# A shift convolution on the two row halves of TensorE's array, with one constant loaded later and some copies assigned by hand

## The chip, the cores and the metric

One core of one Trainium2 chip runs the whole program. The metric is device time in microseconds of one execution; the median of three runs is given, and one further execution was taken with the profiler. Engines are named as in the profile: PE is TensorE (PEld its weight loads), DVE is VectorE, ACT is ScalarE, POOL is GpSimd, SP is SyncE, which here only issues DMAs.

## The reference

The program computes four residual layers over a sequence of S = 2048 rows and D = 448 channels, and all gradients. Only the first kind of layer matters here:

```python
def _A_ref(q, k, v, shift_k, ssm_k, ssm_D):
    k_shift = jnp.zeros_like(k)
    for t in range(ks):                                   # ks = 4
        k_shift = k_shift + k_pad[:, t:t + S, :] * shift_k[:, ks - 1 - t][None, None, :]
    kv = k_shift * v
    y = irfft(rfft(kv) * rfft(ssm_k))[:S]                 # long causal convolution, by channel
    y = y + kv * ssm_D
    return q * y
x = x + A(layernorm(x)); x = x + B(layernorm(x)); x = x + A(layernorm(x)); x = x + B(layernorm(x))
```

`kv` and `y` don't depend on x, so they are computed once, in a prefix, and used by both A layers.

## The kernel before

**Stages.** `_ssm_prefix` computes `y` (tile Ysb) and stores what the backward pass needs: KS_d (the shifted k), and SPEC_d (the two spectra, of K and of KV). `Main.run` does the four layers and their backward pass in four chunks of 512 rows, with an order for PE written out by hand. `_ssm_suffix` does the backward pass of the convolution, with weight gradients (`Jobs`) woven in.

**The prefix**, in program order:

1. SP loads, one behind the other: the filter K in four parts (ksb), the constant M1sb in two halves, k (kn), v (vn), the first rows of x (x0c0), Gsb, Gpre, and Minvsb (1 MB, `_load_minv`, L389), which is first used by `ys` (L594), the last step of the prefix.
2. `k_turn` (L399) transposes K on PE, 16 transposes for 128 channels, and copies the result from PSUM in two halves. Which engine copies is chosen by `bal.pick`, which keeps a running sum of work given to ACT and DVE. `k_stage1` (L409) is the first FFT stage, four matmuls and one cast for each pair of rows.
3. The diagonals (L426): for each of 4 channel blocks of 112 and each of 4 taps, DVE scales the identity by the tap's column, so that a matmul with the result multiplies each channel by its tap. The taps are loaded by ACT's queue (skb) and cast to FP32 on POOL (skc).
4. SP turns two pieces of the K spectrum by DMA (L439) and, behind them, w2 (L449, L450), whose tile takes the place of kn.
5. k is transposed on PE (ps_kT, L445), 4 blocks of 112 channels for each of 16 row groups, and copied to kT by ACT (blocks 0 and 1) and DVE (blocks 2 and 3).
6. `conv(h, jq)` (L453): for half h of the channels (224) and four row groups, 4 x 2 x 4 = 32 matmuls of a 112x128 piece of kT with a 112x112 diagonal, four taps accumulated. ACT casts the result to SBUF (ks), POOL stores it to KS_d, DVE multiplies it with v (kvt). `stage1_kv` (L472) is the first FFT stage of kvt, two steps behind conv. Between them stand the turns of K's spectrum (h = 0) or `spec_k` (h = 1): the second FFT stage of K, its store to SPEC_d and four copies on POOL's queue that swap halves (KAB<-KAB).
7. The products, in the order of the string PRODUCTS, which fixes PE, ACT, DVE and POOL: second stages (P, F), turns of KV (Z), spectra products (M), inverse stages (V), casts, and on POOL the stores of both spectra. Two of the stores are followed by the loads of w1 (L556) and w2 (L562).
8. `ys` (L588) makes Ysb. `Main.run` weaves it with the first transposes and matmuls; the first chunk's X (L716) is written into the buffer that ZkvB had (tag WX), Ysb into that of ZkvA (tag W2).

**Rules that set the order.** PE, ACT and DVE copies of one PSUM tile run one after the other. `issue_after(i)` keeps what follows behind instruction i in the order of issue. A tile with the tag of an earlier one waits until all users of that one, DMAs included, are through. Each engine issues its DMAs in order; POOL's wait for earlier ones of its own to land before they reuse a semaphore. PSUM tag "A" has four buffers of two banks (4 KB in each partition).

`GBLK`, which exists before, is the list of channel blocks (0, 128), (128, 256), (256, 384), (320, 448): the last two overlap, and rows 64 to 127 of the last are channels 384 to 447.

Of the kernel before, what the change touches and what calls it, by code (L numbers as in the profile page):

```python
# [10 lines left out]
FP32 = mybir.dt.float32  # L11
BF16 = mybir.dt.bfloat16
# [5 lines left out]
P = 128  # L18
# [124 lines left out]
def kernel(  # L143
# [197 lines left out]
def _ssm_prefix(k):  # L341
# [4 lines left out]
    with ExitStack() as es:  # L346
# [19 lines left out]
        diag = w2o[:DC, 2 * S:].rearrange("p (c j d) -> p c j d", c=ND, j=4)  # L366
        kn = k.wk.tile([P, J, D], BF16, name="k_n", tag="WY")
        vn = k.wk.tile([P, J, D], BF16, name="v_n", tag="WB")
        skc = spec.tile([DC, ND, 4], FP32, name="skc")
        skb = spec.tile([DC, ND, 4], BF16, name="skb")  # L370
# [69 lines left out]
        for jq in range(4):  # L440
            pt = psum.tile([DC, ND, 4, P], BF16, name="ps_kT", **a_)
# [9 lines left out]
        DH = D // 2  # L451

        def conv(h, jq):  # L453
            ds = slice(h * DH, (h + 1) * DH)
            pc = psum.tile([P, 4, 256], FP32, name="ps_cv", tag="A", bufs=4)
            for u in range(4):
                j = 4 * jq + u
                for e in range(2):
                    for t in range(4):
                        js = (j - t) % J  # L460
                        src = kT[:, js // 4, 2 * h + e, js % 4, 1:129] if j >= t else kT[:, js // 4, 2 * h + e, js % 4, 0:128]
                        nc.tensor.matmul(pc[:, u, e * DC:(e + 1) * DC], lhsT=src, rhs=diag[:, 2 * h + e, t, :], start=(t == 0), stop=(t == 3))
            kk = work.tile([P, 2, 4, DH], BF16, name="ks_kv", tag="pab", bufs=4)
            ks, kvt = kk[:, 0], kk[:, 1]
# [3 lines left out]
            nc.vector.tensor_tensor(out=kvt, in0=ks, in1=vn[:, 4 * jq:4 * jq + 4, ds], op=ALU.mult)  # L468
            bal.add("dve", 0.62)
            return kvt  # L470

        def stage1_kv(h, jq, kvt):  # L472
            for u in range(0, 4, 2):
                n2 = 4 * jq + u
                ps = psum.tile([P, 2, 2, 256], FP32, name="ps_s1", **k.pt["s1"])
                for w in range(2):
                    for c in range(2):
                        nc.tensor.matmul(ps[:, w, c, :DH], lhsT=k.M1sb[:, n2 + w, c, :], rhs=kvt[:, u + w, :], start=True, stop=True)
                _copy(nc, bal.pick(4 * DH), A1kv[:, 112 * h:112 * (h + 1), :, n2:n2 + 2, :].rearrange("p b c w s -> p w c b s"),
                      ps[:, :, :, :DH].rearrange("p w c (b s) -> p w c b s", s=2))  # L480

# [713 lines left out]
def _ssm_suffix(k):  # L1195
# [8 lines left out]
    with ExitStack() as es:  # L1204
# [73 lines left out]
        for cp in range(NCI // 2):  # L1278
# [18 lines left out]
            if cp == 5:  # L1297
                ksf = sp.tile([P, 2, J, D // 2], BF16, name="ksf")
                with tc.issue_after(k.last_x.ins):
                    nc.scalar.dma_start(out=ksf[:], in_=k.KS_d[:].rearrange("h p j d -> p h j d"))  # L1300
# [24 lines left out]
        for i in range(8):  # L1325
# [8 lines left out]
            nc.vector.tensor_tensor(out=gks[:, sl, :], in0=gkv, in1=gks[:, sl, :], op=ALU.mult)  # L1334
            nc.vector.tensor_tensor(out=gkv.rearrange("p j (h d) -> p j h d", h=2), in0=gkv.rearrange("p j (h d) -> p j h d", h=2), in1=ksf[:, :, sl, :].rearrange("p h j d -> p j h d"), op=ALU.mult)
            nc.gpsimd.dma_start(out=out3_pm[:, sl, :], in_=gkv)
# [98 lines left out]
```

## Time and profile before

| | us |
|---|---|
| median of three runs (694.54 to 697.23) | 696.32 |
| profiled execution | 694.42 |
| its span, first to last instruction | 692.5 |
| PE busy | 672.4 (97%) |
| DVE / ACT / POOL busy | 481.5 / 429.2 / 104.6 |
| one conv on PE (32 matmuls) | 1.74 |
| first ps_y on PE | 86.0 |
| first matmul of the first layer's ps_h | 97.6 |

A line of the order of time gives start and duration in us, engine, line of the kernel, operation, tile written and tiles read, shape, count, and in brackets the engine's idle time before it and what ended that. A line of the table by stretch gives the stretch and its length, busy time and number of instructions of PE, PEld, DVE, ACT and POOL, TensorE's granted clock, the share of the 16 DMA engines in use and what they moved in GB/s; the share counts packets by their durations, so overlapping packets can take it above 1. The prefix in stretches of four microseconds begins so, and its first loads keep the DMA engines full:

```profile
0.00:4.00 4.00, 2.81 (x7) 1.01 (x8) 0.27 (x1) 1.49 (x2) 1.74 (x9) 1.00 0.40 127
4.00:8.00 4.00, 4.00 (x36) 3.03 (x35) 2.67 (x15) 0.00 (x0) 0.20 (x1) 1.00 1.03 360
...
16.00:20.00 4.00, 3.72 (x46) 3.29 (x45) 3.73 (x4) 4.00 (x6) 0.00 (x0) 1.00 1.00 411
...
24.00:28.00 4.00, 3.48 (x124) 3.13 (x122) 1.94 (x4) 3.63 (x3) 0.59 (x1) 1.00 1.47 167
28.00:32.00 4.00, 2.62 (x62) 2.46 (x62) 2.23 (x4) 2.92 (x4) 0.55 (x1) 0.84 0.99 252
```

### The profile page before, as it was taken

To read this page: it belongs to the slowest core of one execution; us is meant where nothing else is said; L and a number is where in the kernel's file an instruction comes from. 1 tells how busy PE (TensorE), PEld (TensorE's weight loads), DVE (VectorE), ACT (ScalarE), POOL (GpSimd) and SP (SyncE) were. 2 spreads that over 40 slices of the span, in tenths; PEclk is the share of its full clock that TensorE was granted. 3 is DMA by queue.
4 is the path that set the end of the run, shared out by engine and by line. 5 is a ranking of instruction groups with operands and counts; after the bars stand their busy time and mean duration, and the time that the engine had idled before them with its cause. 6 is when DMAs were issued, how large, how long until landed. Compare 5 with 4: busy or idle time off the path is not lost.

```text
span 692.5 us, 14496 instructions
## 1 busy us (share of the span) xinstructions
PE 672.4 (97%) x5879; PEld 363.3 (52%) x5879; DVE 481.5 (70%) x1131; ACT 429.2 (62%) x522; POOL 104.6 (15%) x177
## 2 busy tenths in 40 slices
PE   8899999899999999999999999999999999999997
PEld 6886845454434444444444444544554555555666
DVE  6579943667889858899478874843946555538992
ACT  5888976968847858669577685223543554554431
POOL 1057310110011100111000100010111211102311
PEclk9999999999999999999999999999999999999999
DMA  8999978269789877498666789949599988956981
GB/s 314 282 277 307 345 205 205 77 169 271 175 251 240 216 185 182 132 250 226 193 156 189 204 198 369 273 160 214 185 249 316 355 274 316 351 186 221 315 315 42
DMA packets 203956, 162.60 MB, mean 235 GB/s; under 512 B 153505, under 2 KB 184244, under 8 KB 203122
## 3 DMA queue, kind: packets, MB, share of 16 engines
q1 hardware_dynamic: 190806, 113.35, 60.2%
q0 software_dynamic: 11088, 39.84, 16.6%
q10 hardware_dynamic: 1996, 8.49, 3.6%
q8 instruction: 46, 0.75, 0.4%
q14 instruction: 20, 0.16, 0.1%
HBM read 66.05 MB, written 54.60 MB: 174 GB/s over the span
## 4 chain that ended last, share of the span: by engine, by line
PE 64%; DVE 18%; issue 6%; DMA 5%; ACT 4%; POOL 3%; POOLq 0%; ACTq 0%
PE ps_d L1077 24%; PE ps_n L867 8%; PE ps_h L669 6%; PE ps_g L669 6%; PE ps_o L829 5%; DVE ln_st L308 2%; DVE lb_v L1025 2%; PE ps_v L272 2%; POOL rstd L313 2%; DMA spec_KV<-ZkvB 1%; DVE n L316 1%; DVE lb_v L1028 1%; DVE lb_v L1029 1%; DVE X L833 1%; PE ps_h L673 1%
## 5 line engine op out<-in xcount | busy, mean ns | idle before, releaser
L1077 PEld LDWEIGHTS <-dstat 128*128 128x128 bf16 x928 | 87.0, 98 | 76.2 <-issue 4.0
L867 PE MATMUL ps_n<-w1T,ghT 128*128 128x448 bf16 x448 | 96.6, 353 | 2.0 <-DVE ghT L852 1.7
L829 PE MATMUL ps_o<-w2sb,aT 128*128 128x448 bf16 x448 | 89.2, 353 | 0.6 <-DVE X L833 0.6
L669 PE MATMUL ps_h<-nT,w1sb 128*128 128x512 bf16 (+1 forms) x420 | 84.4, 337 | 1.6 <-ACT Dall L116 1.0
L116 ACT CAST ghT<-ps_g 128x1024 bf16<-128x1024 f32 (+1 forms) x54 | 48.4, 899 | 58.3 <-PE ps_g L673 46.6
L669 PE MATMUL ps_g<-nT,w2T 128*128 128x512 bf16 x336 | 79.5, 379 | 1.0 <-DVE Dall L117 0.5
L867 PEld LDWEIGHTS <-ghT 128*128 128x128 bf16 x448 | 41.5, 98 | 50.6 <-DVE ghT L852 6.7
L829 PEld LDWEIGHTS <-aT 128*128 128x128 bf16 x448 | 43.2, 98 | 41.1 <-issue 2.7
L669 PEld LDWEIGHTS <-w1sb 128*128 128x128 bf16 x420 | 39.2, 98 | 36.7 <-issue 7.2
L812 ACT ACTIVATE aT<-ps_h 128x1024 bf16<-128x1024 f32 (+1 forms) x48 | 44.2, 921 | 19.4 <-PE ps_h L669 12.2
L116 ACT CAST Dall<-ps_h 128x1024 bf16<-128x1024 f32 (+2 forms) x60 | 54.3, 904 | 0.0
L1025 DVE SCALAR_TENSOR_TENSOR lb_v<-lb_u,n 128x448 bf16<-128x448 bf16 x60 | 37.2, 620 | 24.5 <-ACT lb_u L871 24.1
L313 POOL TENSOR_TENSOR rstd<-ln_ve,mhalf 128x2 f32<-128x2 f32 (+1 forms) x24 | 19.9, 831 | 225.3 <-DVE ln_ve L312 225.3
L669 PEld LDWEIGHTS <-w2T 128*128 128x128 bf16 x336 | 31.3, 98 | 42.0 <-issue 7.2
L822 ACT ACTIVATE Dall<-Dall 128x1024 bf16<-128x1024 bf16 (+1 forms) x48 | 53.3, 1186 | 0.1
L1077 PE MATMUL ps_d<-X,dstat 128*128 128x448 bf16 x224 | 47.6, 353 | 0.2 <-DMA dstat<-a_d 0.2
L1077 PE MATMUL ps_d<-go,dstat 128*128 128x448 bf16 x224 | 47.2, 353 | 0.0
L1077 PE MATMUL ps_d<-n3m,dstat 128*128 128x448 bf16 (+1 forms) x240 | 47.0, 340 | 0.0
L1077 PE MATMUL ps_d<-n1m,dstat 128*128 128x448 bf16 (+1 forms) x240 | 46.5, 340 | 0.0
L871 ACT ACTIVATE lb_u<-ps_n,rstd 128x448 bf16<-128x448 f32 x32 | 20.5, 640 | 28.7 <-PE ps_n L867 24.3
L116 ACT CAST A1g<-ps_v 128x1024 bf16<-128x1024 f32 x14 | 15.1, 1079 | 36.8 <-PE ps_v L272 36.8
L833 DVE TENSOR_TENSOR X<-X,ps_o 128x448 bf16<-128x448 bf16 x32 | 19.5, 610 | 21.3 <-PE ps_o L829 21.1
(210 smaller groups left out, 1114.2 us busy)
## 6 DMA issues: line engine op xcount, KB each, us to landing
dstat<-a_d SPq DMA_DIRECT2D x28, 512.0 KB, 5.1
dstat<-g_d SPq DMA_DIRECT2D x28, 512.0 KB, 5.0
a_d<-turned SPq DMA_DIRECT2D x16, 512.0 KB, 3.0
g_d<-turned SPq DMA_DIRECT2D x16, 512.0 KB, 3.0
a_d<-turned SPq DMA_DIRECT2D x16, 384.0 KB, 2.7
g_d<-turned SPq DMA_DIRECT2D x16, 384.0 KB, 3.2
spec_K<-KAB POOLq DMA_DIRECT2D x7, 512.0 KB, 5.2
KAB<-KAB POOLq DMA_DIRECT2D x28, 128.0 KB, 5.0
```

Source lines behind the costliest of these rows:

```text
L116: return nc.scalar.copy(out, in_)
L272: nc.tensor.matmul(pv[:, r ^ (ci & 1), i, :], lhsT=src[ri, i * P:(i + 1) * P], rhs=k.Gsb[ri, g, ri], start=first, stop=not first)
L313: nc.gpsimd.tensor_tensor(out=r[:, lo:hi], in0=ve[:, lo:hi], in1=k.mhalf[:, lo:hi], op=ALU.pow)
L669: self.nc.tensor.matmul(ps, lhsT=w[:, b, ft * P:(ft + 1) * P], rhs=x[:, b], start=(start and b == 0), stop=(stop and b == bs[2]))
L812: self.last_silu = nc.scalar.activation(aT[hh][:, o:o + hi - lo, :], ps(lo, hi), ACT.Silu)
L822: self.nc.scalar.activation(dT[hh][:, o:o + n, :], dT[hh][:, o:o + n, :], ACT.Derivative_silu)
L829: nc.tensor.matmul(po[:, :D], lhsT=aT[ft // 7][:, ft % 7, tl * P:(tl + 1) * P], rhs=self.w2sb[:, ft, :], start=(ft == 0), stop=(ft == NF - 1))
L833: self.last_o = nc.vector.tensor_tensor(out=X[:, t, :], in0=X[:, t, :], in1=po[:, :D], op=ALU.add)
L867: nc.tensor.matmul(pn[:, :D], lhsT=gh[ft // 7][:, ft % 7, tl * P:(tl + 1) * P], rhs=self.w1T[:, ft, :], start=(ft == 0), stop=(ft == NF - 1))
L871: nc.scalar.activation(u0[:], pn[:, :D], ACT.Identity, scale=k.rstd[2 * L + 1][:, t:t + 1], accum_out=cp[:, tl, 0:1])
L1025: nc.vector.scalar_tensor_tensor(out=v[:], in0=u0, scalar=-1.0 / D, in1=n_t, op0=ALU.mult, op1=ALU.mult, accum_out=cp[:, 1:2])
L1077: self.nc.tensor.matmul(ps[:, cols], lhsT=st[:, t, :], rhs=mov[:, t, cols], start=(first and t == 0), stop=(last and t == NT - 1))
```

## The change

- **conv** now has two parts of 256 and 192 channels. Channels stand in the blocks of `GBLK`, and each matmul takes 64 of them: rows 0 to 63 or 64 to 127 of kT with a 64x64 diagonal. Part 0 has 64 matmuls, the row halves alternating; part 1 has 48, since block 3 only needs its rows 64 to 127. The two row halves write different banks of ps_cv. The cast to ks puts the columns back into channel order (part 0), or takes three of the four column groups (part 1).
- **The diagonals** are made by two products of the identity with the taps, both operands broadcast, on DVE behind the last copy of `k_turn`. skc and its cast are gone; the taps come in two DMAs.
- **k_turn's copies**: first half on DVE, second on ACT, without `bal.pick`.
- **Minvsb** is loaded by SP behind w2's turns.
- **KS_d** is one [128, 16, 448] array; each conv stores pieces of 256 or 192 channels. The suffix reads it back as one tile.
- `stage1_kv` works on parts of 256 and 192 channels.

```diff
-    k.KS_d = dram.tile([2, P, J, D // 2], BF16, name="KS_d")
+    k.KS_d = dram.tile([P, J, D], BF16, name="KS_d")
...
-        kT = k.wk.tile([DC, 4, ND, 4, 129], BF16, name="kT", tag="W1")
-        w2o = k.wk.tile([P, 2 * S + ND * 4 * DC], BF16, name="ksd", tag="W2")
+        kT = k.wk.tile([P, 4, ND, 4, 129], BF16, name="kT", tag="W1")
+        w2o = k.wk.tile([P, 2 * S + ND * 4 * 64], BF16, name="ksd", tag="W2")
...
-        nc.scalar.dma_start(out=skb[:], in_=k.A_shift_k.rearrange("(c p) j -> p c j", p=DC))
+        nc.scalar.dma_start(out=skb[:, 0:3, :], in_=k.A_shift_k[0:384, :].rearrange("(c p) j -> p c j", p=P))
+        nc.scalar.dma_start(out=skb[64:128, 3, :], in_=k.A_shift_k[384:448, :])
...
-        _load_minv(k, nc.sync)
...
-        nc.gpsimd.tensor_copy(skc[:], skb[:])
...
-            for g in range(2):
-                _copy(nc, bal.pick(8 * n, dve_ns=0.53), Kt[:, 8 * g:8 * g + 8, lo:hi], pv[:, g])
+            for g, e in enumerate((nc.vector, nc.scalar)):
+                last = _copy(nc, e, Kt[:, 8 * g:8 * g + 8, lo:hi], pv[:, g])
+                bal.add("act" if g else "dve", 0.9 if g else 0.69)
+                if g == 0:
+                    k.kt_copy = last
...
-        for dc in range(ND):
-            for j in range(4):
-                nc.vector.tensor_scalar(out=diag[:, dc, j, :], in0=k.ident[:DC, :DC], scalar1=skc[:, dc, j:j + 1], scalar2=None, op0=ALU.mult)
-        bal.add("dve", 3.0)
+        with tc.issue_after(k.kt_copy.ins):
+            for r, n in ((0, 3), (1, 4)):
+                rs = slice(64 * r, 64 * r + 64)
+                nc.vector.tensor_tensor(out=diag[rs, 0:n].rearrange("p c j d -> p (c j) d"),
+                                        in0=k.ident[rs, rs].rearrange("p (o d) -> p o d", o=1).broadcast_to((64, 4 * n, 64)),
+                                        in1=skb[rs, 0:n].rearrange("p c (j o) -> p (c j) o", o=1).broadcast_to((64, 4 * n, 64)), op=ALU.mult)
+        bal.add("dve", 2.0)
...
-                    nc.tensor.transpose(pt[:, dc, u, :], kn[:, j, dc * DC:(dc + 1) * DC], k.ident[:])
+                    nc.tensor.transpose(pt[:, dc, u, :], kn[:, j, GBLK[dc][0]:GBLK[dc][1]], k.ident[:])
...
-        nc.sync.dma_start_transpose(out=k.w2T[:, 3:4, :], in_=k.B_w2[:, 320:448])
+        w2t = nc.sync.dma_start_transpose(out=k.w2T[:, 3:4, :], in_=k.B_w2[:, 320:448])
+        with tc.issue_after(w2t.ins):
+            _load_minv(k, nc.sync)
+        CH = ((0, 256), (256, 448))
...
-            pc = psum.tile([P, 4, 256], FP32, name="ps_cv", tag="A", bufs=4)
+            lo, hi = CH[h]
+            w = hi - lo
+            pc = psum.tile([P, 4, 4, 64], FP32, name="ps_cv", tag="A", bufs=4)
+            at = {(0, 0): 0, (0, 1): 2, (1, 0): 1, (1, 1): 3} if h == 0 else {(2, 0): 1, (2, 1): 2, (3, 1): 3}
...
-                        nc.tensor.matmul(pc[:, u, e * DC:(e + 1) * DC], lhsT=src, rhs=diag[:, 2 * h + e, t, :], start=(t == 0), stop=(t == 3))
+                        for r in range(2):
+                            if (e, r) in at:
+                                rs = slice(64 * r, 64 * r + 64)
+                                nc.tensor.matmul(pc[:, at[e, r], u, :], lhsT=src[rs], rhs=diag[rs, e, t, :], start=(t == 0), stop=(t == 3))
...
-            nc.scalar.copy(ks, pc[:, :, :DH])
-            bal.add("act", 0.95)
-            nc.gpsimd.dma_start(out=k.KS_d[h, :, 4 * jq:4 * jq + 4, :], in_=ks)
+            if h == 0:
+                nc.scalar.copy(ks.rearrange("p u (e r d) -> p r e u d", e=2, r=2), pc[:].rearrange("p (r e) u d -> p r e u d", r=2))
+            else:
+                nc.scalar.copy(ks.rearrange("p u (x d) -> p x u d", x=3), pc[:, 1:4])
+            bal.add("act", 0.85)
+            nc.gpsimd.dma_start(out=k.KS_d[:, 4 * jq:4 * jq + 4, lo:hi], in_=ks)
...
-                ksf = sp.tile([P, 2, J, D // 2], BF16, name="ksf")
+                ksf = sp.tile([P, J, D], BF16, name="ksf")
```

More of the change, by code (lines that the diff above doesn't have):

```diff
@@ L440, in _ssm_prefix @@
         for jq in range(4):
-            pt = psum.tile([DC, ND, 4, P], BF16, name="ps_kT", **a_)
+            pt = psum.tile([P, ND, 4, P], BF16, name="ps_kT", **a_)
             for u in range(4):
@@ L456, in conv @@
             for u in range(4):
                 j = 4 * jq + u
-                for e in range(2):
+                for e in (2 * h, 2 * h + 1):
                     for t in range(4):
                         js = (j - t) % J
-                        src = kT[:, js // 4, 2 * h + e, js % 4, 1:129] if j >= t else kT[:, js // 4, 2 * h + e, js % 4, 0:128]
-                        nc.tensor.matmul(pc[:, u, e * DC:(e + 1) * DC], lhsT=src, rhs=diag[:, 2 * h + e, t, :], start=(t == 0), stop=(t == 3))
@@ L463, in conv @@
-            kk = work.tile([P, 2, 4, DH], BF16, name="ks_kv", tag="pab", bufs=4)
-            ks, kvt = kk[:, 0], kk[:, 1]
-            nc.scalar.copy(ks, pc[:, :, :DH])
-            bal.add("act", 0.95)
-            nc.gpsimd.dma_start(out=k.KS_d[h, :, 4 * jq:4 * jq + 4, :], in_=ks)
-            nc.vector.tensor_tensor(out=kvt, in0=ks, in1=vn[:, 4 * jq:4 * jq + 4, ds], op=ALU.mult)
+                        src = kT[:, js // 4, e, js % 4, 1:129] if j >= t else kT[:, js // 4, e, js % 4, 0:128]
+                        for r in range(2):
+                            if (e, r) in at:
+                                rs = slice(64 * r, 64 * r + 64)
+                                nc.tensor.matmul(pc[:, at[e, r], u, :], lhsT=src[rs], rhs=diag[rs, e, t, :], start=(t == 0), stop=(t == 3))
@@ new lines, in conv @@
+            kk = work.tile([P, 2, 4, 256], BF16, name="ks_kv", tag="pab", bufs=4)
+            ks, kvt = kk[:, 0, :, :w], kk[:, 1, :, :w]
+            if h == 0:
[4 more added lines that the diff above has]
+            nc.gpsimd.dma_start(out=k.KS_d[:, 4 * jq:4 * jq + 4, lo:hi], in_=ks)
@@ L469, in conv @@
+            nc.vector.tensor_tensor(out=kvt, in0=ks, in1=vn[:, 4 * jq:4 * jq + 4, lo:hi], op=ALU.mult)
             bal.add("dve", 0.62)
@@ L477, in stage1_kv @@
                     for c in range(2):
-                        nc.tensor.matmul(ps[:, w, c, :DH], lhsT=k.M1sb[:, n2 + w, c, :], rhs=kvt[:, u + w, :], start=True, stop=True)
-                _copy(nc, bal.pick(4 * DH), A1kv[:, 112 * h:112 * (h + 1), :, n2:n2 + 2, :].rearrange("p b c w s -> p w c b s"),
-                      ps[:, :, :, :DH].rearrange("p w c (b s) -> p w c b s", s=2))
+                        nc.tensor.matmul(ps[:, w, c, :w_], lhsT=k.M1sb[:, n2 + w, c, :], rhs=kvt[:, u + w, :], start=True, stop=True)
+                _copy(nc, bal.pick(4 * w_), A1kv[:, lo // 2:hi // 2, :, n2:n2 + 2, :].rearrange("p b c w s -> p w c b s"),
+                      ps[:, :, :, :w_].rearrange("p w c (b s) -> p w c b s", s=2))
         def spec_k(cp):
@@ L1297, in _ssm_suffix @@
             if cp == 5:
-                ksf = sp.tile([P, 2, J, D // 2], BF16, name="ksf")
+                ksf = sp.tile([P, J, D], BF16, name="ksf")
                 with tc.issue_after(k.last_x.ins):
-                    nc.scalar.dma_start(out=ksf[:], in_=k.KS_d[:].rearrange("h p j d -> p h j d"))
+                    nc.scalar.dma_start(out=ksf[:], in_=k.KS_d[:])
                 skx = ws[:, 0:8 * D].rearrange("p (a b) -> p a b", a=2)
@@ L1334, in _ssm_suffix @@
             nc.vector.tensor_tensor(out=gks[:, sl, :], in0=gkv, in1=gks[:, sl, :], op=ALU.mult)
-            nc.vector.tensor_tensor(out=gkv.rearrange("p j (h d) -> p j h d", h=2), in0=gkv.rearrange("p j (h d) -> p j h d", h=2), in1=ksf[:, :, sl, :].rearrange("p h j d -> p j h d"), op=ALU.mult)
+            nc.vector.tensor_tensor(out=gkv, in0=gkv, in1=ksf[:, sl, :], op=ALU.mult)
             nc.gpsimd.dma_start(out=out3_pm[:, sl, :], in_=gkv)
```

9 lines of the change are left out of this document (4 added, 5 removed).

## The prediction

> **What bounds the kernel now.** The change touches the prefix (0 to about 98 us) and one load and one product near the end. After about 100 us the chain of waits runs mostly through PE, so I ask what lets the main part begin. First view: DVE's order of time at the end of the prefix.
>
> ```profile
> 87.97 0.62 DVE L715 TENSOR_TENSOR a_t<-na,Ysb 128x896 bf16<-128x896 bf16 x1 [0.91 <-ACT Ysb L595]
> 89.19 0.63 DVE L716 TENSOR_TENSOR X<-x0c,a_t 128x896 bf16<-128x896 bf16 x1 [0.59 <-DMA spec_KV<-ZkvB]
> ...
> 92.76 0.70 DVE L316 TENSOR_SCALAR n<-X,ln_mv,rstd 128x448 bf16<-128x448 bf16 x2
> ```
>
> X shares a buffer (tag WX) with ZkvB, so its first write waits until ZkvB's last store to HBM has landed. X then gates the norm, and n at 93.46 gates the transposes (L657) that PE runs at 93.59, straight after a ps_g that is done at 93.59. So two chains end within 0.15 us of each other: the **engine chain** (casts to A1kv, ps_y from 86.0, Ysb, ps_g) and the **store chain**. Second view: the stores of tile spec_KV, their line on landing times, and POOL's order of time.
>
> ```profile
> DMA to landing us min/median/max: 4.4/7.3/12.2
> ```
> ```profile
> 75.33 0.78 POOL L556 DMA_DIRECT2D w1sb<-in_B_w_dram  x1 [1.16 <-PE ps_v L261]
> 76.10 0.58 POOL L557 DMA_DIRECT2D w1sb<-in_B_w_dram  x1
> 76.80 0.55 POOL L551 DMA_DIRECT2D spec_KV<-ZkvB  x1
> ```
>
> The last ZkvB store is issued at 76.80 behind w1sb's 1.8 MB, and 76.80 + 12.2 = 89.0, where L716 starts (89.19). Third view: DMA by stretch; the last two columns are the share of the 16 DMA engines and GB/s.
>
> ```profile
> 40.00:42.00 2.00, 1.73 (x21) 1.33 (x20) 1.36 (x5) 2.00 (x3) 1.61 (x2) 1.00 1.12 319
> 42.00:44.00 2.00, 2.00 (x31) 1.51 (x28) 1.99 (x2) 1.02 (x2) 0.46 (x1) 1.00 0.76 305
> 44.00:46.00 2.00, 1.78 (x26) 1.57 (x25) 1.74 (x3) 2.00 (x4) 2.00 (x5) 1.00 0.68 262
> 46.00:48.00 2.00, 2.00 (x27) 1.52 (x25) 0.79 (x2) 1.93 (x4) 2.00 (x5) 1.00 0.95 237
> 48.00:68.00 20.00, 18.29 (x186) 12.36 (x185) 18.63 (x20) 16.79 (x18) 14.16 (x29) 1.00 0.95 303
> 68.00:89.00 21.00, 19.70 (x298) 16.12 (x296) 18.55 (x19) 19.12 (x22) 7.42 (x13) 1.00 1.01 352
> ```
>
> From 48 us until X may be written the DMA engines are full; they idle only in 42 to 48 us. Whatever the engines save, the store chain moves only by what the DMA saves.
>
> **The engine chain.** (1) Convolution. Now 32 matmuls of 112x112 per call, 1.74 us; the new form, 64 channels on alternating row halves, has an exact counterpart late in the kernel:
>
> ```profile
> 37.91 1.74 PE L462 MATMUL ps_cv<-ksd,kT 112*128 112x112 bf16 x32
> ```
> ```profile
> 531.26 1.11 PE L272 MATMUL ps_v<-Gsb,pab 64*128 64x64 bf16 x64
> ```
>
> The 256-channel part has 4 x 4 x 2 x 2 = 64 of these: 1.11 us, 0.63 saved, four times 2.5. The 192-channel part has 48, of which 16 (block 3) have no partner: 32 x 17 ns = 0.55, and 16 at 17 ns (0.28) up to today's 54 ns (0.87); I take 35 ns, one half alone at half the paired rate: 1.11 us, again 0.63 (bounds 0.32 to 0.91), 2.5 for four. Together 5.0 us of PE. The Trainium skill, "TensorE: Matmul & The Clock Gate", section "Wait — 56ns, not 53.3ns?", says matmuls never start closer than about 25 ns: 64 would then take 1.6 us and the saving nearly vanish. This trace shows 17 ns on row halves, so the trace decides.
>
> (2) What of it arrives. In 22.6 to 39.5 us (h=0) PE is busy 15.0 of 16.9, ACT 12.84, DVE 10.62; in 39.5 to 53.4 (h=1) 12.73 of 13.9, 11.91 and 10.82. With 2.5 less on PE, ACT becomes the fuller one in both: h=0 can give 2 to 4, h=1 at most 13.9 - 11.9 = 2.0. I take 2 + 2 = 4. PE's pause of 1.90 us at 27.48, with the half clock behind it (a conv at 31.05 takes 3.16), has no releaser; I assume that it stays. The casts keep their element counts (2 x 896 become 1024 + 768; 0.91 us now), the kT copies their 1024 per lane.
>
> (3) Diagonals. 14 + 2 tensor_scalars (2.31 + 0.40 us) leave 5.33 to 8.56, where DVE's first turn copy waited for them (7.56, though its 16 transposes were through near 6.8). The second turn's transposes end at 8.18 in any case, and ps_s at 9.21 follows its copy: gain 0.25. Two broadcast products of 768 and 1024 per lane come back behind the last turn copy (14 us): at the pab product's rate (1.22 us for 2048) 1.06, at the PSUM cast's (1.22 for 1024) 2.1. DVE is busy 8.75 of 10 us there, so they are hardly hidden; nearest is the second rate, as one input steps by zero. Against it ACT has one cast less after 14.45 (0.8) and the half-size last copy (0.55) more. Net price 0.7 (bounds -0.3 to 1.3). skc's cast on POOL and its wait fall away; off the path.
>
> Sum of (1) to (3): ps_y 4 - 0.7 = 3.3 us earlier (bounds 0.7 to 5.7).
>
> **The store chain.** (a) Holes. spec_K's first store (43.54) comes with the engine chain; then 42 to 48 us has no hole: 2 x (0.24 + 0.32 + 0.05) = 1.2 us gained. Lower bound 0; upper 2.2, if 48 to 68 goes from 0.95 to 1.00 too.
> (b) Minvsb, 1 MB, leaves 12.15 to 26.5 (14.3 us to landing). Behind it on SP's queue stand K's two turns, w2's two, and gb0. The first turn's issue takes 6.13 us, the second's 3.57; the 2.56 between them is 1 MB at the 411 GB/s of 16 to 20 us, so the turns wait for Minvsb and move up by it. Minvsb then lands near 42 and gb0 near where it did (43.6); ps_y and ps_t read them after 82. The 1 MB costs 2.56 to 3.0 us (at 352 GB/s) in the new place and frees 2.56: net 0 to 0.45, I take 0.1. Without that cover: +2.6 to 3.0.
> (c) KS_d's 8 stores of 224 KB go out in pieces of 512 and 384 bytes instead of 1792. Nearest row: POOL's stores of wts, 112 KB in 256-byte pieces, land in 5.0 us, those of dout, 112 KB in 896-byte rows, in 5.4: no extra (lower bound 0). Upper: the turns, moved in 256-byte pieces, ran at 167 GB/s in 24 to 28 us, and 1.83 MB at 167 instead of 352 is 11.0 - 5.2 = +5.8. I take 0.3. POOL's issue grows from 0.58 to about 0.8 (w1sb's 384 rows take 0.78); POOL waits for landings between them, which hides it.
>
> Sum: -1.2 + 0.1 + 0.3 = **-0.8 us**. The engine chain's 3.3 is more than this, so 2.5 of it becomes a longer wait at L716. ksf has the same bytes (8.6 us to landing) and its product the same 896 elements (0.616 us): 0. 694.42 us for the profiled execution (span 692.5 plus 1.9) becomes 693.6. The median shown is 1.9 above that execution: **695.5 us**.
>
> **The rivals.**
> 1. *The stores move with the engines*: before 42 us the turns show a DMA share above 1, so their lanes overlap, and earlier stores may slip in between for nothing. Then the engine chain decides: 696.3 - 3.3 = 693.0 (690.6 to 695). Against it: full DMA from 48 us on.
> 2. *KS_d's small pieces* (slower): POOL's queue is one line, so each slow KS_d store delays the spec_K and KAB copies behind it and in the end L716's landing. It decides once the pieces cost over 1.2 of their 5.2 us, 23%; at half rate 5.8 - 1.2 = +4.6, **700.9**; for the 384-byte ones alone (0.79 MB, +2.5) 697.6. For it: the rate of the turns; against it: wts. The Trainium skill, "DMA: Bandwidth & Descriptors", section "Specifications", states that transfers under 512 bytes are read, modified and written, which by an estimate at half rate is this rival for the 384-byte stores; wts' landing time disagrees.
> 3. *Minvsb isn't given back*: if K's and w2's turns end at 42 as now, being bound by their own rate, its 2.6 to 3.0 fall into the full stretch: -1.2 + 2.8 + 0.3 = +1.9, 698.2. Against it: 6.13 beside 3.57.
>
> **How the numbers follow.** Forecast 0.46 (own range 694.1 to 697.0, from bounds -2.2 and +0.7), rival 1 0.30, rival 2 0.13, rival 3 0.11. A measurement of this kernel tells about 0.5%, 3.5 us: faster means below 692.8, slower above 699.8. Faster: 0.18 of rival 1 and 0.02 of the forecast, 0.20. Slower: 0.09 of rival 2 and 0.03 of rival 3, 0.12. The rest, 0.68, is within. The range cuts rival 1 at 691.0 and rival 2 at 699.5.
>
> **What would show it.** Right: a conv of 64 near 1.1 us, of 48 near 1.1; no diagonal before the first turn copy; spec_K's first store before 42; DMA share near 0.95 from 42 to 48; L716 still waiting for spec_KV, now over 1 us, and starting near 88.4; ps_y near 82.7. Wrong: L716 starting with its a_t (rival 1), KS_d landing well over its 4.2 us (rival 2), w2's turn still ending near 42 and gb0 near 46 (rival 3), or a conv over 1.5 us. A different order of DVE or ACT work after 100 us would make me wrong in a way that none of this covers.

## The result, and the profile after

| | before | after |
|---|---|---|
| median of 20 runs, us | 694.84 (692.41 to 699.38) | 699.22 (696.68 to 702.89) |
| profiled execution (its span), us | 694.42 (692.5) | 697.92 (695.9) |
| matmuls of conv | 256 | 448 |
| first to last conv on PE | 22.60 to 50.41 | 25.17 to 53.87 |
| first store of spec_K issued | 43.54 | 46.82 |
| last store of ZkvB issued | 76.80 | 80.39 |
| first ps_y | 86.03 | 89.11 |
| X written (L716, now L732) | 89.19 | 93.19 |
| first ps_h | 97.60 | 101.54 |

The ratio is 1.0056, 95% interval [1.0043, 1.0068]: the changed kernel is slower by 0.56%, a little more than the 0.5% that the prediction took as the least that a measurement of this kernel tells. From the first ps_h to the end it takes 594.3 us, before 594.9; in every run below this stretch lies between 594.3 and 595.1 us. All that the change does, it does in the prefix, and the column to read is the last line of the table: 3.94 us later.

Three answers of the trace of after, to be held against those of the prediction. First DVE's order of time where X is written (start, duration, and in brackets the idle time before and what ended it):

```profile
91.05 0.62 DVE L731 TENSOR_TENSOR a_t<-na,Ysb 128x896 bf16<-128x896 bf16 x1 [1.14 <-ACT Ysb L611]
93.19 0.62 DVE L732 TENSOR_TENSOR X<-x0c,a_t 128x896 bf16<-128x896 bf16 x1 [1.52 <-DMA spec_KV<-ZkvB]
```

POOL's order of time, with the last store of ZkvB behind w1sb's two loads, and the landing times of tile spec_KV, here over the whole run with the later loads from it (up to 130 us, as in the prediction, they are 5.3, 7.0 and 12.6):

```profile
78.31 0.78 POOL L572 DMA_DIRECT2D w1sb<-in_B_w_dram  x1 [0.22 <-PE ps_v L261]
79.08 0.57 POOL L573 DMA_DIRECT2D w1sb<-in_B_w_dram  x1
80.39 0.54 POOL L567 DMA_DIRECT2D spec_KV<-ZkvB  x1 [0.74 <-ACT A1kv L116]
```
```profile
DMA to landing us min/median/max: 3.9/6.7/12.6
```

And the DMA engines by stretch (the last two columns are their share and GB/s):

```profile
22.00:24.00 2.00, 2.00 (x39) 2.00 (x37) 1.16 (x2) 1.59 (x3) 0.00 (x0) 1.00 0.04 14
42.00:44.00 2.00, 2.00 (x57) 1.68 (x56) 0.98 (x2) 2.00 (x3) 0.72 (x1) 1.00 1.05 439
44.00:46.00 2.00, 1.82 (x11) 0.97 (x11) 1.93 (x5) 2.00 (x3) 1.18 (x3) 1.00 0.96 393
46.00:48.00 2.00, 1.41 (x52) 1.08 (x50) 1.89 (x3) 1.49 (x2) 1.87 (x4) 1.00 0.74 260
48.00:68.00 20.00, 18.37 (x242) 12.63 (x244) 17.37 (x20) 17.83 (x20) 15.29 (x29) 1.00 0.96 299
```

The store chain still ends last, now by 1.52 us in place of 0.59: 80.39 + 12.6 = 93.0, and L732 starts at 93.19. It is 4.0 us later than before, and most of that it had from its first link: the first spec_K store is issued 3.3 us later, the way from there to the last ZkvB store is 0.3 us longer (33.57 for 33.26), and the landing 0.4 (12.6 for 12.2). That link comes from the engines, so what has to be explained is the engine chain: forecast 3.3 us earlier at ps_y, measured 3.1 later. The stretch 42 to 46 us has no hole any more, but a new one lies at 22 to 24 us (0.04, before 1.03 and 421 GB/s): Minvsb is no longer there, and K's turns, which were to fill its place, are issued at 22.89 us, before at 20.16.

PE's order of time in the conv stage holds the cause; "x43" counts the matmuls of a group that follow the pause, "issue" means that the profile shows nothing that PE waited for:

```profile
25.17 1.11 PE L473 MATMUL ps_cv<-ksd,kT 64*128 64x64 bf16 x64
...
27.13 0.48 PE L473 MATMUL ps_cv<-ksd,kT 64*128 64x64 bf16 x21
29.80 0.80 PE L473 MATMUL ps_cv<-ksd,kT 64*128 64x64 bf16 x43 [2.19 <-issue]
...
34.23 0.53 PE L473 MATMUL ps_cv<-ksd,kT 64*128 64x64 bf16 x13 [0.68 <-DVE KAB L117]
35.72 1.54 PE L473 MATMUL ps_cv<-ksd,kT 64*128 64x64 bf16 x51 [0.97 <-issue]
...
41.37 0.57 PE L473 MATMUL ps_cv<-ksd,kT 64*128 64x64 bf16 x27 [0.31 <-issue]
...
42.85 1.11 PE L473 MATMUL ps_cv<-ksd,kT 64*128 64x64 bf16 x48
...
47.56 0.48 PE L473 MATMUL ps_cv<-ksd,kT 64*128 64x64 bf16 x15 [0.59 <-issue]
```

The same view of before has one such pause, with slow matmuls behind it:

```profile
29.38 0.80 PE L232 MATMUL ps_tr<-ident,KAB 64*128 64x64 bf16 x43 [1.90 <-issue]
30.11 1.11 PE L478 MATMUL ps_s<-ks_kv,M1sb 128*128 128x224 bf16 x8
31.05 3.16 PE L462 MATMUL ps_cv<-ksd,kT 112*128 112x112 bf16 x32
```

A conv of 64 takes 1.11 us, one of 48 too: the saving per call is there. But there are four pauses without a releaser, 4.06 us in sum, where before had one of 1.90; and the granted clock is half from 31.2 to 41.4 us, before from 30.7 to 34.2. The extra 6.8 us at half clock are worth some 3.4 us of PE work, the longer pauses 2.2: with these 5.6 us the 5.0 that the convs save are spent. The stage takes 28.7 us, before 27.8.

**Where the pauses lie.** They cut groups in the middle, and always after the same number of matmuls. From the first to the second: 43 of the conv, 64 transposes, 8 of ps_s and 13 of the next conv, 128. From the second to the third: 51 + 32 + 8 + 37 = 128. From the third to the fourth 127 are recorded. With its weight load each matmul is two instructions, so a pause comes every 256 instructions of PE (the last one is 2 short, by the matmul that isn't recorded). The page of after has what belongs to that:

```profile
PE 669.5 (96%) x6035; PEld 360.0 (52%) x6071; DVE 481.5 (69%) x1117; ACT 429.9 (62%) x522; POOL 105.8 (15%) x176
...
q8 instruction: 47, 0.77, 0.4%
```

0.77 MB in 47 packets is 16 KB each, and over PE's 6035 + 6071 instructions 64 bytes each: 256 to a packet. (Before: 5879 + 5879 instructions, 46 packets, 0.75 MB.) The Trainium skill, "Perfetto Trace Analysis", section "The 4-stage abstract model", calls an instruction 64 bytes, and the trace agrees. So this queue carries PE's program, and a pause lies where one packet ends and the next isn't there yet. By the trace's records of this queue the packets of after start at 27.40, 33.40, 38.84 and 45.08 us, and the pauses end 2.3 to 2.5 us behind them. And they start late: PE goes on at 29.80, 35.72 and 41.37 us, and only 3.6, 3.1 and 3.7 us after each of these does the next packet start. So from one of these places to the next it takes such a delay and the 2.3 to 2.5 us together, 5.9, 5.7 and 6.2 us, though PE's work from the first to the second was through in 4.9 (29.80 to 34.75). 128 matmuls on row halves at 17 ns take 2.2 us, 128 of the old ones at 54 ns 7.0: the smaller the matmuls, the sooner PE is at the end of its packet.

### The profile page after: what moved, and what is told of

Same layout as the page of the kernel before. It is cut to its first block, busy times and chain, and to the rows that moved or that the text cites. A ratio compares the mean times of both kernels' runs of the same rounds, so it can differ in the third digit from the quotient of the medians.

```text
span 695.9 us, 14830 instructions
## 1 busy us (share of the span) xinstructions
PE 669.5 (96%) x6035; PEld 360.0 (52%) x6071; DVE 481.5 (69%) x1117; ACT 429.9 (62%) x522; POOL 105.8 (15%) x176
## 4 chain that ended last, share of the span: by engine, by line
PE 64%; DVE 18%; issue 6%; DMA 5%; ACT 4%; POOL 3%; POOLq 0%; DVEq 0%; ACTq 0%
PE ps_d L1093 25%; PE ps_n L883 8%; PE ps_h L685 6%; PE ps_o L845 5%; PE ps_g L685 5%; DVE ln_st L308 3%; DVE lb_v L1041 2%; PE ps_v L272 2%; DMA spec_KV<-ZkvB 2%; POOL rstd L313 2%; DVE n L316 1%; DVE lb_v L1044 1%; DVE lb_v L1045 1%; DVE X L849 1%; PE ps_h L689 1%
## 5 line engine op out<-in xcount | busy, mean ns | idle before, releaser
L685 PE MATMUL ps_g<-nT,w2T 128*128 128x512 bf16 x317 | 77.9, 380 | 2.2 <-DVE Dall L117 0.5
L883 PEld LDWEIGHTS <-ghT 128*128 128x128 bf16 x448 | 41.4, 98 | 50.7 <-DVE ghT L868 6.7
L887 ACT ACTIVATE lb_u<-ps_n,rstd 128x448 bf16<-128x448 f32 x32 | 20.5, 639 | 28.7 <-PE ps_n L883 24.3
```

The costliest lines, as they stand in the source:

```text
L685: self.nc.tensor.matmul(ps, lhsT=w[:, b, ft * P:(ft + 1) * P], rhs=x[:, b], start=(start and b == 0), stop=(stop and b == bs[2]))
L883: nc.tensor.matmul(pn[:, :D], lhsT=gh[ft // 7][:, ft % 7, tl * P:(tl + 1) * P], rhs=self.w1T[:, ft, :], start=(ft == 0), stop=(ft == NF - 1))
L887: nc.scalar.activation(u0[:], pn[:, :D], ACT.Identity, scale=k.rstd[2 * L + 1][:, t:t + 1], accum_out=cp[:, tl, 0:1])
```

## The experiments

Each ratio is to the kernel before on the same chip. "Pauses" are those of PE without a releaser between 22 and 56 us, of 0.3 us or more, in sum; "half" is the time at half clock between 10 us and the first ps_h. Before has 1.90 and 3.4.

| run | ratio [95%] | conv matmuls | pauses | half | ps_y | X | ps_h |
|---|---|---|---|---|---|---|---|
| after | 1.0056 [1.0043, 1.0068] | 448 | 4.06 | 17.1 | 89.11 | 93.19 | 101.54 |
| e1_minv_back | 1.0058 [1.0032, 1.0084] | 448 | 5.43 | 13.7 | 91.21 | 96.50 | 104.86 |
| e2_diag_late | 1.0035 [1.0008, 1.0062] | 448 | 3.96 | 13.6 | 90.48 | 95.12 | 103.47 |
| e3_both | 1.0066 [1.0044, 1.0088] | 448 | 7.61 | 10.2 | 89.86 | 94.97 | 103.33 |
| e4_before_minv_late | 1.0036 [1.0009, 1.0063] | 256 | 0.58 | 6.8 | 83.66 | 90.04 | 100.87 |
| e5_late_blocks | 1.0052 [1.0038, 1.0066] | 256 | 0 | 0 | 89.97 | 92.57 | 101.54 |
| e6_before_split | 1.0096 [1.0076, 1.0116] | 512 | 6.30 | 10.2 | 93.53 | 98.42 | 106.78 |
| e7_before_ksd | 1.0020 [1.0001, 1.0039] | 256 | 2.13 | 3.4 | 86.15 | 90.88 | 99.24 |
| e8_minv_late_w1_last | 0.9967 [0.9955, 0.9979] | 256 | 0 | 0 | 83.70 | 86.30 | 95.27 |
| e9_before_w1_last | 0.9979 [0.9962, 0.9996] | 256 | 2.12 | 3.4 | 86.05 | 88.65 | 97.62 |
| e10_after_w1_last | 1.0045 [1.0025, 1.0065] | 448 | 5.13 | 3.4 | 89.44 | 92.04 | 101.01 |
| e11_hybrid | 0.9988 [0.9973, 1.0003] | 320 | 0 | 3.4 | 86.10 | 88.69 | 97.67 |
| e12_plain_turns | 1.0030 [1.0007, 1.0052] | 448 | 2.10 | 3.4 | 85.82 | 89.04 | 97.40 |
| e13_halves_all | 1.0034 [1.0023, 1.0045] | 448 | 5.66 | 6.8 | 88.65 | 91.24 | 100.22 |
| e14_hybrid_copies | 0.9999 [0.9987, 1.0011] | 320 | 0 | 0 | 85.29 | 87.90 | 96.87 |

The columns of times are of one profiled execution each, and a single one can stray from its median by an us or more: that of after lies 1.3 us below it, e2's 2.2 above, e12's 2.8 below (so a later ps_h in e2 goes with no larger ratio). The ratios decide.

**Parts of the change undone: Minvsb's place, the diagonals, both.** e1_minv_back:

```diff
+        _load_minv(k, nc.sync)
...
-        with tc.issue_after(w2t.ins):
-            _load_minv(k, nc.sync)
```


> The changed kernel with Minvsb loaded behind Gpre again. Changed kernel: 1.0056 of before (+3.9 us). Theory D (the diagonals on DVE hold up L414, PE pauses 1.59 us and its clock halves, K's first stage ends 22.9 instead of 20.2): Minvsb's load isn't the cause, 0 to -1 us, ratio 1.004 to 1.0056. Theory M (Minvsb's 1 MB no longer fills the loads' queue, DMA share 0.04 in 22 to 24 us, and comes back in the full stretch): -2.5 to -3 us, ratio about 1.002. Theory P (more PE instructions are fetched while the DMA turns run, PE pauses and its clock is half from 31 to 41 us): 0, ratio 1.0056.

e2_diag_late puts the diagonals behind DVE's last cast of K's first stage:

```diff
-        with tc.issue_after(k.kt_copy.ins):
+        with tc.issue_after(k.s1_dve.ins):
```


> The changed kernel with the two diagonal products on DVE behind the last cast of K's first stage instead of behind the last turn copy. Theory D: L414 follows the last turn copy, no pause of PE, clock full until 27 us, K's first stage ends near 20, about -2.7 us, ratio about 1.0015. Theory M: the gap at 22 to 24 us closes too, since K's turns start near 20, but Minvsb still comes late: -2 at most. Theory P: 0 to -1, since the pauses and the half clock of 31 to 41 us stay.

e3_both has both edits:

> Both of these: Minvsb behind Gpre, diagonals behind K's first stage. Theories D and M together: about -4 to -5 us from the changed kernel, ratio 0.998 to 1.000, the last spec_KV landing near 88.5. Theory P: no better than 1.003, since what conv costs is left.

Undoing the load gains nothing here (e1 1.0058, e3 1.0066), and PE's pauses get longer, 4.57 and 3.04 us in e3. Moving the diagonals is worth something: K's first turn is issued at 21.47 us for 22.89, and the ratio is 1.0035, though its interval and that of after overlap. What they cost at their place in after, by the orders of time of DVE and PE:

```profile
12.54 0.94 DVE L430 TENSOR_TENSOR ksd<-ident,skb 64x768 bf16<-64x768 bf16 x1
13.40 1.80 DVE L117 CAST KAB<-ps_s 128x768 bf16<-128x768 f32 x2
15.14 0.24 DVE L414 TENSOR_TENSOR KAB<-KAB,Drow 1x192 bf16<-1x192 bf16 x1
```
```profile
15.43 6.23 PE L417 MATMUL ps_s<-KAB,M1sb 128*128 128x192 bf16 x36 [1.59 <-DVE KAB L414]
```

The first product stands before two casts, and L414, of 0.24 us, behind all three. PE waits 1.59 us for it; within that wait the clock goes to half (14.1 to 20.9), and 36 matmuls take 6.23 us that took 3.68 before:

```profile
13.91 3.68 PE L416 MATMUL ps_s<-KAB,M1sb 128*128 128x192 bf16 x36 [0.52 <-DVE KAB L117]
```

(e10 and e12 have the same wait of 1.59 us, and the full clock behind it.) e1, e2 and e3 all keep 448 matmuls, long pauses, and a ratio over 1; if the load's place and the diagonals were the whole cause, e3 would have come out at 0.998 to 1.000.

**One part of the change alone, on the kernel before.** e4_before_minv_late moves only Minvsb:

```diff
-        _load_minv(k, nc.sync)
...
+        with tc.issue_after(w2t.ins):
+            _load_minv(k, nc.sync)
```


> The kernel before with only Minvsb's load moved behind w2's turns. The prediction's cover (K's and w2's turns move up by 2.56 us): 0 to +0.5 us, ratio 1.000 to 1.001. Theory M: +2.5 to +3 us, ratio 1.004. Theory D and P: 0.

The engines gain by it: conv ends at 48.03 (50.41), ps_y starts at 83.66 (86.03). X comes only 0.85 us later. Yet the run is slower, and PE's order of time behind X shows by what:

```profile
94.07 1.23 PE L658 MATMUL ps_t<-ident,n 128*128 128x128 bf16 x8 [2.85 <-DVE n L316]
95.09 3.19 PE L595 MATMUL ps_y<-A1kv,Minvsb 128*128 128x448 bf16 x8
```

PE, done early, waits 2.85 us for the norm of X; from within that wait on the clock is half for 6.8 us (93.4 to 100.2), and ps_h starts 10.83 us after X where it was 8.41. X itself is late for its engines: the first spec_K store goes out 2.3 us earlier (41.23), the last ZkvB store 0.75 later (77.55), so the store chain between them grew by 3.1 us.

e6_before_split changes nothing but the number of matmuls: each one of conv is cut into two of 56 columns, with the same products, stores and loads as before.

```diff
-                    for t in range(4):
+                    for c, t in [(c, t) for c in (0, 56) for t in range(4)]:
...
-                        nc.tensor.matmul(pc[:, u, e * DC:(e + 1) * DC], lhsT=src, rhs=diag[:, 2 * h + e, t, :], start=(t == 0), stop=(t == 3))
+                        nc.tensor.matmul(pc[:, u, e * DC + c:e * DC + c + 56], lhsT=src, rhs=diag[:, 2 * h + e, t, c:c + 56], start=(t == 0), stop=(t == 3))
```


> The kernel before with every conv matmul cut into two of 56 columns: 512 instead of 256 of them, the same products. Theory P: pauses of 4 to 7 us in the conv stage, half clock for 7 to 14 us, X's first write 3 to 6 us later, ratio 1.004 to 1.008. Rival R: the array's time is the same (56 columns take about 27 ns, twice that is today's 54), so 0 to +0.5 us, ratio 1.000 to 1.001.

A conv takes 1.81 us for 1.74 where nothing holds it up, so eight cost 0.6 us more. The run is 1.0096, its stage 35.8 us long for 27.8:

```profile
24.91 0.72 PE L462 MATMUL ps_cv<-ksd,kT 112*128 112x56 bf16 x21
29.17 1.54 PE L462 MATMUL ps_cv<-ksd,kT 112*128 112x56 bf16 x43 [3.53 <-issue]
...
41.01 1.42 PE L462 MATMUL ps_cv<-ksd,kT 112*128 112x56 bf16 x27 [2.77 <-issue]
```

The pauses sit at x43 and x27 as in after; between them are 256 matmuls. 4.4 us of pauses more, 6.8 us more at half clock (some 3.4 us of work) and the 0.6 make 8.4: about the 8.0 that the stage grew.

e7_before_ksd takes only KS_d's layout over, with pieces of 448 bytes for 1792:

```diff
-            nc.gpsimd.dma_start(out=k.KS_d[h, :, 4 * jq:4 * jq + 4, :], in_=ks)
+            nc.gpsimd.dma_start(out=k.KS_d[:, 4 * jq:4 * jq + 4, ds], in_=ks)
```


> The kernel before with only KS_d's layout changed to one array of 448 channels per row, so that its stores go out in pieces of 448 instead of 1792 bytes. If small pieces cost DMA time: POOL's issue 0.8 instead of 0.58 us, landings later, X's first write 1 us later or more, ratio 1.0015 or more (rival 2 of the prediction: 1.002 to 1.007). Theory P: no difference, 0.999 to 1.001.

conv and ps_y stay within 0.2 us; POOL's issue of a store grows from 0.58 to 0.80 us, the last ZkvB store goes out at 78.34 (76.80), and X waits 2.17 us for 0.59: 1.7 us later on the store chain alone, 0.2% in time. POOL's longer issues are not what comes through: the last KS_d store goes out at 53.81 (53.95), and the chain falls back by 1.5 us only at the sixth spec_K store (64.41 for 62.48), behind a landing of KAB that POOL waits 2.24 us for. That the small pieces delayed this landing isn't shown. The Trainium skill, "DMA: Bandwidth & Descriptors", section "Specifications", asks for at least 512 bytes and says that less is read, modified and written; the run's interval agrees, barely, that it costs, and doesn't show by which way.

**Blocks in place of row halves.** e5_late_blocks is e2 with 128x128 diagonals, 32 matmuls in each conv:

```diff
-                        for r in range(2):
-                            if (e, r) in at:
-                                rs = slice(64 * r, 64 * r + 64)
-                                nc.tensor.matmul(pc[:, at[e, r], u, :], lhsT=src[rs], rhs=diag[rs, e, t, :], start=(t == 0), stop=(t == 3))
+                        rs, m = (slice(64, 128), 64) if e == 3 else (slice(0, 128), 128)
+                        o = 128 * (e % 2)
+                        nc.tensor.matmul(pc[:, u, o:o + m], lhsT=src[rs], rhs=diag[rs, e, t, 0:m], start=(t == 0), stop=(t == 3))
```


> e2_diag_late with conv in whole blocks: 128x128 diagonals, 32 matmuls per call in both parts (block 3 on its upper half), 256 in all as in the kernel before, instead of 64 and 48, 448 in all; parts of 256 and 192 channels, KS_d, Minvsb and the diagonals' place as in e2. Theory P (PE runs out of instructions while the DMA turns keep the queues full, and its clock halves behind that): PE's unexplained pauses in the conv stage fall from 5.8 us to about 2 as in the kernel before, the half clock from 13.6 us to one window of 3.4, the last conv ends near 50 instead of 55, about -3 us against e2, ratio 0.999 to 1.001. Rival R (the pauses come from the DMA turns and from where Minvsb and KS_d stand, whatever the number of matmuls): as e2, 1.0035.

No pause without a releaser, no half clock; but a conv takes 1.95 us (256 channels) and 2.25 (192), 16.8 in sum for 13.9 before, and the stage is 31.0 us long. The cause of the pauses is gone, and the gain it was paid for too: that is why the ratio isn't the 0.999 to 1.001 that was expected of it.

**The store chain taken away.** e8, e9 and e10 issue w1sb's loads behind the last spec_KV store, on e4, on before and on after:

```diff
-                    if lo == 6:
+                    if lo == 9:
```


> e4_before_minv_late (Minvsb behind w2's turns, all else as before) with the loads of w1 issued behind the last store of spec_KV instead of before it. If the store chain's end is set by w1's 1.8 MB in front of that store: X no longer waits for spec_KV, its first write comes with Ysb near 86.2, PE has no pause of 2.85 us before ps_t and no half clock, ps_h starts near 95.2 instead of 97.6 (before) or 100.9 (e4), ratio 0.9955 to 0.998. Rival: ps_h then waits for w1sb, or the DMA's total sets the end: no better than 1.000.

> The kernel before with w1's loads behind the last store of spec_KV, Minvsb where it was. If both chains end together in the kernel before, taking the store chain away alone gives next to nothing: X follows Ysb, ps_y still starts at 86.0 because PE's pause of 1.9 us at 27.5 stays, ratio 0.9985 to 1.000; and what e8 gained (0.9967) came from Minvsb's late load too, which shortens that pause. If the store chain alone was the bound: as e8.

> The changed kernel with w1's loads behind the last store of spec_KV. Of the changed kernel's +3.9 us, ps_y's later start (89.1 instead of 86.0) is the engine chain, 3.1; the rest, at most 1.5 (X's wait for spec_KV), is the store chain. Theory P: -0.5 to -1.5 us, ratio 1.003 to 1.0045. If the store chain was the whole of it: ratio 1.000 or less.

In all three X starts with its a_t (0.03 us of idle time). e8 is the fastest kernel of this study, 692.31 us, 0.9967 [0.9955, 0.9979], and beats both; e9 reaches 0.9979 by w1 alone, better than expected. Its profiled execution doesn't show where: X comes 0.5 us earlier, but ps_h stays at 97.62 (97.60), as the prediction's two chains that end within 0.15 us would have it. For after it is worth 0.5 us at ps_h, and 1.0045 remains: without a store chain the changed kernel is still slower, by its engines.

**The DMA turns.** e12_plain_turns puts plain copies in the place of K's and w2's four turns, so this kernel leaves these transpositions out:

```diff
-            nc.sync.dma_start_transpose(out=Z[:, 16 * g:16 * g + 16, :], in_=A1Kf[:, 16 * g:16 * g + 16, :].rearrange("p a b -> p (a b)"))
+            nc.sync.dma_start(out=Z[:, 16 * g:16 * g + 16, :], in_=A1Kf[:, 16 * g:16 * g + 16, :])
...
-        nc.sync.dma_start_transpose(out=k.w2T[:, 0:3, :], in_=k.B_w2[:, 0:384])
+        nc.sync.dma_start(out=k.w2T[:, 0:2, :].rearrange("p a f -> p (a f)"), in_=k.minv_h.ap()[:, 0:2 * F])
```


> The changed kernel with K's two DMA turns and w2's two replaced by plain copies of as many bytes (which leaves out these transpositions). Theory P as stated (PE's instruction fetch is starved while the turns' 256-byte pieces fill the queues): PE's pauses of 2.19, 0.97 and 0.59 us in conv vanish or fall below 0.5 us, and the half clock of 31 to 41 us with them; the last conv ends near 49. If the rate of instructions alone is too high for PE's fetch: the pauses stay at 2 us and more in sum.

The pauses at x43 and x51 are shorter (1.44 and 0.66), those at x27 and x15 are gone, and ps_y is at 85.82, 3.3 us earlier than in after. So the turns may have a part in the pauses, but they aren't all of it. How large a part isn't shown: this is the fastest of the kernel's nine executions (693.73 us, median 696.55), the intervals of e12 and after overlap, and e10, with the turns and the same conv, lost its pauses at x51 and x15 too.

**The count of matmuls with all else mended.** e11_hybrid has 128x128 blocks in the part of 256 channels (32 matmuls of 1.95 us), row halves in the part of 192 (48 of 1.11), late diagonals, KS_d as two arrays and w1sb last:

```diff
+                        if h == 0:
+                            nc.tensor.matmul(pb[:, u, 128 * e:128 * e + 128], lhsT=src, rhs=dgb[:, e, t, :], start=(t == 0), stop=(t == 3))
+                            continue
...
-            nc.gpsimd.dma_start(out=k.KS_d[:, 4 * jq:4 * jq + 4, lo:hi], in_=ks)
+            nc.gpsimd.dma_start(out=k.KS_d[h][:, 4 * jq:4 * jq + 4, :], in_=ks)
```


> Changed kernel with: row halves only in the 192-channel part, which runs after the turns have landed; the 256-channel part in whole 128x128 blocks (320 matmuls in all instead of 448); diagonals behind K's first stage; KS_d as two arrays, stored in pieces of 2048 and 1536 bytes, and read back into two parts with two products; w1's loads behind the last store of spec_KV. Theory P: no unexplained pause over 1 us, no half clock, ps_y near 84 or earlier, ratio 0.993 to 0.998. If row halves lose also without the turns: pauses of 0.5 us or more in each of the four later convs, ratio over 1.000.

e13_halves_all takes the three added lines out again, so that both parts run on row halves (with the diagonals and the cast to ks that belong to them):

> This is the hybrid with one part changed back: the part of 256 channels is convolved in 64 matmuls of 64x64 on row halves as in the changed kernel, not in 32 with 128x128 blocks (448 matmuls in all for the hybrid's 320). Diagonals late, w1 behind the last spec_KV store, KS_d in two arrays, as in the hybrid. Theory P (more PE instructions run into pauses without a releaser while the DMA turns run, with half clock behind them): PE pauses with no releaser of 2 us or more in sum between 22 and 50 us, where the hybrid has none, ps_y at 88 to 90 us (hybrid 86.1), ratio 1.002 to 1.005. Rival (the matmuls' number is not the cause; what made the changed kernel late is the diagonals, KS_d and the store chain, all of them mended here): no such pauses, the conv of 64 takes 1.1 us for 1.95, ps_y at 84 to 86, ratio 0.995 to 0.999.

PE's order of time, first of e13, then of e11:

```profile
27.69 0.80 PE L476 MATMUL ps_cv<-ksd,kT 64*128 64x64 bf16 x43 [2.32 <-issue]
...
33.61 1.42 PE L476 MATMUL ps_cv<-ksd,kT 64*128 64x64 bf16 x51 [1.17 <-issue]
...
40.36 0.71 PE L476 MATMUL ps_cv<-ksd,kT 64*128 64x64 bf16 x27 [2.17 <-issue]
```
```profile
22.87 1.95 PE L476 MATMUL ps_cv<-ksd,kT 128*128 128x128 bf16 x32 [0.23 <-ACT kT L116]
...
32.76 3.13 PE L476 MATMUL ps_cv<-ksd,kT 128*128 128x128 bf16 x32 [1.79 <-DVE KAB L117]
```

This settles it. e13's convs need 4 x (1.95 - 1.11) = 3.4 us less of PE than e11's, and its stage is 2.4 us longer (30.4 for 28.0): 5.66 us of pauses at x43, x51 and x27, none in e11. ps_y is 2.55 us later, the ratio 1.0034 [1.0023, 1.0045] for 0.9988 [0.9973, 1.0003]. The instruction packets start at the same times in both (25.37 and 31.04, 25.34 and 30.95) while PE has 703 and 933 instructions behind it in e13, 553 and 805 in e11: e13 gets to the end of its packets before the next one comes.

e14_hybrid_copies goes after the 1.79 us for which e11's PE waits for DVE's copy of K's transposes; it gives these copies to the engines of before:

```diff
-                _copy(nc, bal.pick((hi - lo) * P, dve_ns=0.53), o.rearrange("p i (r x) -> p r i x", r=2), pt[:, :, lo:hi, :])
+                e = nc.scalar if g < 2 else nc.vector
+                bal.add("act" if g < 2 else "dve", 1.91 if g < 2 else 1.25)
+                _copy(nc, e, o.rearrange("p i (r x) -> p r i x", r=2), pt[:, :, lo:hi, :])
```


> The hybrid, with the PSUM copies of K's transposes (tag ps_tr) given to the engines as in the kernel before: the first two to ACT, the last three to DVE. Theory (the 1.79 us for which PE waits for DVE's KAB copy comes from the balancer's other choice): that pause is 0.7 us or less, the conv stage ends about 1 us earlier (last conv before 50.2), ps_y at 84.3 to 85.5 (hybrid 86.1), ratio 0.995 to 0.998. Rival (another engine takes the pause's place, or DVE is the bound there): pause or its like stays, ps_y within 0.4 of 86.1, ratio as the hybrid's 0.9988.

The pause stays at 1.79 us. Of the five copies the edit moves only the third (ACT at 30.18 in e11, DVE at 31.80 here), so that one's engine isn't the cause; the first two are on ACT in both. In DVE's order the copy (31.80) stands behind the product ks_kv (30.66), which waits for ACT's cast of ps_cv (29.58), and that stands behind two copies of 1.82 us on ACT. No half clock follows here, and ps_y is 0.8 us earlier than in e11; the ratio, 0.9999 [0.9987, 1.0011], is not better. Whether the pause goes when one of these two copies leaves ACT wasn't run.

## Why the prediction came out as it did

**The chains at the end of the prefix.** Right in form: X waits for ZkvB's last store (so not rival 1), now for over 1 us (1.52). But the longer wait was to come from engines 3.3 us early; it came from both chains being late, ps_y by 3.1 us and the store chain by 4.0, so this sign came true by luck. L732 starts at 93.19 and not near 88.4, since that chain's first link hangs on the engines, and these came later. The base was off as well: the forecast put the median 1.9 us above the profiled execution, and over 20 runs it is 0.4 above.

**(1) The size of a conv.** Right: 1.11 us for 64 and for 48 (the 35 ns of a matmul without a partner, an estimate between 17 and 54, was met), and the rate of 17 ns on row halves holds, against the about 25 ns that the Trainium skill, "TensorE: Matmul & The Clock Gate", section "Wait — 56ns, not 53.3ns?", gives as the least.

**(2) What of it arrives: the step that failed.** Of 5.0 us of PE 4 were to arrive, and "PE's pause of 1.90 us at 27.48, with the half clock behind it (a conv at 31.05 takes 3.16), has no releaser; I assume that it stays". It doesn't stay: it is the place where PE's program runs out, and smaller matmuls run it out sooner. Measured: 4.06 us of pauses for the 1.90 and 6.8 us more at half clock, a stage 0.9 us longer, not 4 shorter. e6 makes before slower in this way alone, e13 against e11 does it with all else held but the form of the diagonals and of one cast. The forecast took PE's busy time in the stage as what could be saved; the one line without a releaser in it was the one to follow up. (The upper bound doesn't follow either: h = 0 can't give up to 4 us where PE saves 2.5, and 2.5, 2.0 and the 0.3 of the diagonals make 4.8, not 5.7.)

**(3) The diagonals.** Mis-sized, at their place rather than by their length: the two products take 0.94 and 1.22 us, within the estimate, but the conv stage starts 2.57 us later, not 0.7. The wait for L414 behind the first product, and the half clock around it, were not in the sum. Late diagonals (e13) start the stage at 23.03.

**(a) The holes.** 42 to 46 us was filled as forecast, but by Minvsb and the turns: no spec_K store comes before 46.82, and the hole went to 22 to 24 us.

**(b) Minvsb.** Right for the engines on the kernel before (ps_y 2.4 us earlier in e4), and +0.85 us at X for the 0.1 forecast. In e4 the turns moved up, but the store chain paid for the 1 MB: its 3.1 us more are near rival 3's 2.6 to 3.0, and gb0 lands at 49.5 (37.69 and 11.8), past that rival's sign of 46. In after Minvsb's place wasn't filled, as K's turns came late by (3); gb0 lands at 48.2 (40.53 and 7.7), but the chain from the first spec_K store on is only 0.3 us longer.

**(c) KS_d.** Perhaps mis-sized: 1.7 us at X for 0.3 in e7, in one profiled execution and with pieces of 448 bytes. In after, with pieces of 512 and 384, the store chain grew by 0.3 in all and KS_d's median landing in the prefix is 4.6 us for 4.2, so neither the 1.7 nor the 2.5 of rival 2 is seen there. It was not the cause: with the store chain out of the way (e10) 1.0045 remains.

By steps at ps_h: e13 against e11, the count, 2.55 us; e10 against e13, the early diagonals and the small pieces of KS_d, 0.8; after against e10, the store chain, 0.5. Together 3.85 of the 3.94. These are differences of single profiled executions, and of kernels that come near the changed one by steps, so the split is an estimate; only for the first term do the intervals of the two ratios lie apart.

## What to carry to other kernels

A saving in PE's busy time by more and smaller matmuls has a second price, the program itself: count the instructions per us, look for pauses that the trace gives no releaser, and see whether they fall at a fixed distance in instructions and near packets of the instruction queue. Here PE needed 3.6 to 6.8 us from one such place to the next wherever it paused, so 128 matmuls that are through sooner may gain nothing. A small product put on an engine ahead of a cast costs what waits behind that cast, clock included, not its own length. And a load that is moved out of the way helps only if what stands behind it is ready then: e8 gains with Minvsb late, but only with w1sb moved as well.

## What was not expected of the hardware

- PE's instructions come in packets of 16 KB, and where PE had paused it goes on 2.3 to 3.1 us after such a packet starts (the packet itself takes 0.9 to 1.9 us). Counted in instructions, in all sixteen traces, the first four packets from 25 us on start 0.8 to 4.5 us after PE has passed the place 256 instructions ahead of the one where they are needed. What makes this delay short or long isn't shown, nor what part the DMA turns have in it.
- Pauses and waits of 1.6 to 2.9 us went with half clock in them or behind them, in stretches of 3.4 us or two, three or four times that (3.4 in e10, 6.8 in e4, 10.2 in after, 13.6 in e2). But not always: e14 has a wait of 1.79 us and none. The Trainium skill, "TensorE: Matmul & The Clock Gate", section "What's actually happening", names an idle window of about 3.4 us before the clock is halved; the length of the stretches agrees with that, the shorter pauses don't.
- A delay on one chain can so cost more than its length: in e4 X came 0.85 us later, PE waited 2.85, and ps_h came 3.27 later.
